# Attention and two MLP blocks on one core: bank exits on ScalarE, two-sided values and VectorE sums for batch 3, other group counts

## The chip, the cores and the metric

The kernel runs on one core of a Trainium2 chip. The metric is the device time of one execution in microseconds (us); the median of the runs counts. TensorE does the matmuls, VectorE and ScalarE the elementwise work, GpSimd a little of it, and the DMA issues stand on SyncE's queue (SP).

## What is computed

```python
scores = cap * np.tanh(scale * (q @ k.T) / cap)          # 4 batches, 12 heads, 448 tokens, 64 per head
attn = exp(scores - max(scores)); attn /= sum(attn) + 1e-9
x = attn @ v                                             # heads side by side: 448 x 768
x = x + relu(layer_norm(x) * g_ln @ w_ch1) @ w_ch2       # first MLP, 768 -> 3072 -> 768
u = x + (relu(x.T @ w_tok1) @ w_tok2).T                  # tokens mixed, 448 -> 256 -> 448
y = u + relu(u @ w_ch1) @ w_ch2                          # second MLP, 768 -> 1536 -> 768
```

All of it is float32 at the precision of a split product: an operand is written as a high part in the fp32r form and a low part, and a product is three matmuls (high x high, low x high, high x low).

## The kernel before

Activations lie transposed, with the 768 channels in six blocks of 128 partitions and the 448 tokens of a batch in the free dimension. A planner (`Program`) holds every step with the engines that may do it, an estimated cost and a key; it walks through a simulated time in which each engine takes, of the steps that are ready, the one with the lowest key, and so writes out the order of each engine's queue. The keys come from start times and paces such as `T_ATT3` and `PACE3` (head h of batch 3 has key T_ATT3 + h * PACE3); a lower key goes first, but an engine with nothing else to do takes a later one early.

Order of the work: batch 0's attention and layer norm, batch 1's attention beside one group of batch 0's first MLP alone (N0), and then MLP groups of batches 0 and 1 in pairs, into which batch 2's attention is woven. The first MLP has 6 groups of 512 hidden units, the second 3. A pair group applies the weights of one group to both batches; a lone group loads the same weights for one batch. The groups that are done alone stand beside the token mixing: while one batch is mixed, the other has work. With n lone groups for one batch, the other batch has the same n alone later. N1 is that number for the first MLP of batches 2 and 3, and N2 for the second MLP of both pairs. Batch 3's attention is woven into the token mixing and the second MLP of batches 0 and 1 and has to be done ahead of the pair groups of batches 2 and 3.

Weights come as raw 64-bit words. The first time a group is used, `piece` turns its words into floats and splits them (L272 to L280, two steps on ScalarE, four or five on VectorE), and the split weights are written back to memory; later uses load these (`split<-kept`). Three buffers hold split weights. All loads stand on SP's queue in the planner's order.

A head (`head`, L334): scores to a bank pair (L363), tanh (L366) and exp (L367) on ScalarE, the maxima over queries by a transposed reduction on VectorE (L371, L374). For batches 2 and 3 the exponentials are then split into `eh` and `el` (L389, L391 to L396), 896 columns at a time, and the values too: `vs` holds in 160 columns the high values (64), ones (32) and the low values (64). The values matmuls (L402, L404, L405) add into one bank: rows 0 to 63 are the head's output, rows 64 to 95 the sum of the exponentials, from the ones. The keys come in 3.5 blocks of 128; in the fourth the 64 keys stand twice, and `el` holds there low parts in one half and high parts in the other. L409 takes the sums out of the bank, L412 copies the output to `x`. `divide` gathers sums and maxima of six heads and scales `x`.

The MLP: L563 and L568, L569 (hidden units, split as they leave the bank), L584 and L588 (output, added to `x`). The tokens: L615 to L665. The layer norm: L460 to L508; `normalise`: L516 to L520.

Of the kernel before, what the change touches and what calls it, by code (L numbers as in the profile page):

```python
# [14 lines left out]
AF = mybir.ActivationFunctionType  # L15
# [5 lines left out]
P = 128  # L21
# [36 lines left out]


URGENT, SCORES, PREPARE, LOAD = 1000.0, 19.31, 4.58, 24.58  # L60
N0, N1, N2 = 1, 2, 2
T_LN0, T_LN1 = 7.69, -20.0
T_AHEAD, N_AHEAD, AHEAD_PACE = 14.0, 1, 5.0
T_ALONE, STRETCH0, T_PAIR, STRETCH1 = 85.0, 1.3, 165.0, 1.14
T_ATT2, PACE2, T_ATT3, PACE3 = 171.18, 25.0, 560.0, 30.0
LEAD, RAW_AHEAD, EVACUATE, TOKENS_AHEAD = 6.3, 9.57, -7.49, 17.25


# [80 lines left out]
def block_kernel(ctx: ExitStack, tc: tile.TileContext, qkv, cap, gln, w1, w2, wt1, wt2, con, out):  # L149
# [67 lines left out]

    VS = boxes("vs", 1, [4, DV + D], F32R)
    EH, EL = boxes("eh", 1, [2, S], F32R), boxes("el", 1, [2, S], F32R)
    M = boxes("m", 2, [2, 2, NJ])  # L220
    rs_t, rm_t = [place(f"rs{i}", [H, NJ]) for i in range(2)], [place(f"rm{i}", [H, NJ]) for i in range(2)]
    RS = [[Box(t[:, 6 * g:6 * g + 6]) for g in range(2)] for t in rs_t]
    RM = [[Box(t[:, 6 * g:6 * g + 6]) for g in range(2)] for t in rm_t]
# [101 lines left out]

    def attention(b, start, pace):
        x = x_t[b]
        early = b < 2
        rs, rm = rs_t[b % 2], rm_t[b % 2]
        qks, vls = ring(QK + lent_qk[b]), ring(V + lent_v[b])  # L330
        es = ring(lent if early else OWN)
        ms, scs = ring(M), ring(SC)

        def head(h):  # L334
            grp = h // 6
            pr, hh = divmod(h, 2)
            qk, v, m = next(qks), next(vls), next(ms)
            add("dma", 480, lambda: nc.sync.dma_start(out=qk.at, in_=qkv[b, h, :, :S + 4 * P]), (), [qk], early=LOAD)
            add("dma", 192, lambda: nc.sync.dma_start(out=v.at, in_=qkv[b, h, :, S + 4 * P:].rearrange("p (c d) -> p c d", c=4)), (), [v], early=LOAD)
            q, k = qk.at[:, :S], qk.at[:, S:]  # L340
            if not early:

                (ks,), (qs,), (vs,), (eh,), (el,) = KS, QS, VS, EH, EL
                add("act", 4 * P, lambda: act(ks.at, k, AF.Copy), [qk], [ks], early=PREPARE)  # L344
                add("dve+/pool+", 4 * P, lambda e: low(engine_of[e], ks.at[D:], k[D:], ks.at[D:]), [qk], [ks], early=PREPARE)
                add("act/dve*+", S, lambda e: copy(e, qs.at[:, 0], q), [qk], [qs], early=PREPARE)
                add("dve+/pool+", S, lambda e: low(engine_of[e], qs.at[:, 1], q, qs.at[:, 0]), [qk], [qs], early=PREPARE)

            E = []
            for half in range(2):  # L350
                sc, eb = next(scs), next(es)
                e, eb = eb.at, [eb]
                E.append((e, eb))

                def scores(half=half, sc=sc):
                    for i in range(2):
                        c, rows = 2 * half + i, slice(i * D, (i + 1) * D)
                        if early:

                            mm(sc.at[:, i, :S], k[rows, c * P:(c + 1) * P], q[rows], start=True, stop=True)  # L360
                        else:
                            for j in range(2):
                                mm(sc.at[:, i, :S], ks.at[:, c * P:(c + 1) * P], qs.at[:, j], start=j == 0, stop=j == 1)  # L363

                add("pe", (6 if early else 4) * S, scores, [qk] if early else [ks, qs], [sc], early=URGENT + SCORES)
                add("act", 2 * S, lambda e=e, sc=sc: act(e, sc.at[:, :, :S], AF.Tanh, scale=tsc), [sc], eb)  # L366
                add("act", 2 * S, lambda e=e: act(e, e, AF.Exp, scale=cap_t), (), eb)  # L367

            for half in range(2):
                e, eb = E[half]  # L370
                add("dve", 2 * S, lambda half=half, e=e: dve.tensor_reduce(  # L371
                    m.at[:, half].rearrange("p c j -> p (c j)"), e.rearrange("p c (j i) -> p (c j) i", i=32),
                    axis=AX.X, op=ALU.max, apply_transpose=True), eb, [m])
            add("dve", 4 * NJ, lambda: dve.tensor_reduce(  # L374
                rm[:, h], m.at.rearrange("p a c j -> p j (a c)"), axis=AX.X, op=ALU.max), [m], [RM[b % 2][grp]])
            po = next(head_banks)
            if early:
                def values():
                    for c in range(4):
                        n = P if c < 3 else D  # L380
                        mm(po.at[:DV, :S], v.at[:n, c], E[c // 2][0][:n, c % 2], start=c == 0, stop=c == 3)  # L381

                add("pe", 15 * S, values, [v, *E[0][1], *E[1][1]], [po], early=URGENT)
            else:
                add("act", 4 * D, lambda: act(vs.at[:, :, :D], v.at[:, :, :D], AF.Copy), [v], [vs])
                add("dve+", 4 * D, lambda: low(dve, vs.at[:, :, DV:], v.at[:, :, :D], vs.at[:, :, :D]), [v], [vs])
                for half in range(2):
                    e, eb = E[half]
                    add("act", 2 * S, lambda e=e: act(eh.at, e, AF.Copy), eb, [eh])  # L389
                    if half == 0:  # L390
                        add("dve+", 2 * S, lambda e=e: low(dve, el.at, e, eh.at), [eh, *eb], [el])  # L391
                    else:
                        add("dve+", S, lambda e=e: low(dve, el.at[:, 0], e[:, 0], eh.at[:, 0]), [eh, *eb], [el])

                        add("dve+", S, lambda e=e: dve.scalar_tensor_tensor(
                            el.at[:, 1], eh.at[:, 1].bitcast(F32), neg, e[:, 1], op0=ALU.mult, op1=ALU.add), [eh, *eb], [el])  # L396

                    def values(half=half):
                        for i in range(2):
                            c = 2 * half + i  # L400
                            if c < 3:
                                mm(po.at[:DV, :S], vs.at[:, c, :DV], eh.at[:, i], start=c == 0, stop=False)  # L402
                            n, part = (P, eh) if c < 3 else (D, el)
                            mm(po.at[:D, :S], vs.at[:n, c, DV:], part.at[:n, i], start=False, stop=False)  # L404
                            mm(po.at[:DV, :S], vs.at[:, c, :DV], el.at[:, i], start=False, stop=c == 3)  # L405

                    add("pe", (6 - half) * S, values, [vs, eh, el], [po], early=URGENT)

            add("dve", S, lambda: dve.tensor_reduce(  # L409
                rs[D:DV, h], po.at[D:DV, :S].rearrange("p (j i) -> p j i", i=32),  # L410
                axis=AX.X, op=ALU.max, apply_transpose=True), [po], [RS[b % 2][grp]])
            add("dve", S, lambda: dve.tensor_copy(x[hh * D:(hh + 1) * D, pr], po.at[:D, :S]), [po], [X[b][pr]])  # L412

        def divide(grp):

# [274 lines left out]
    with tc.manual_schedule():  # L690
        setup()
        prog.key = T_AHEAD
        for g in range(N_AHEAD):
            prepare(g)
        prog.key = 0.0
        attention(0, 0.0, 3.97)
        prog.key += T_LN0
        layer_norm(0)
        normalise(0)
        head_banks = side_banks = ring(BANKS[:2])  # L700
        attention(1, 60.01, 6.39)
        prog.key += T_LN1
        layer_norm(1)
        normalise(1)
        head_banks = side_banks = ring(BANKS[:1])

        main_banks = ring(BANKS[2:])
        n0, n1, n2 = N0, N1, N2
        prog.key, stretch = T_ALONE, STRETCH0
        weave(mlp(groups((0,), 0, n0)))  # L710
        main_banks = chain(BANKS[2:], ring(BANKS[1:]))
        attention(2, T_ATT2, PACE2)
        layer_norm(2)
        attention(3, T_ATT3, PACE3)
        prog.key, stretch = T_PAIR, STRETCH1
        weave(mlp(groups((0, 1), n0, NG1 - n0)))
        weave(tokens(0, HIDDEN[2]), mlp(groups((1,), 0, n0)), ahead=TOKENS_AHEAD)
        weave(tokens(1, HIDDEN[2]), mlp(groups((0,), NG1, n2)), ahead=TOKENS_AHEAD)
        weave(mlp(groups((0, 1), NG1 + n2, NG2 - n2), (0,)))
        weave(mlp(groups((1,), NG1, n2), (1,)))  # L720
        normalise(2)
        stretch = 1.0
        weave(mlp(groups((2,), 0, n1)))
        layer_norm(3)
        normalise(3)
        weave(mlp(groups((2, 3), n1, NG1 - n1)))
        weave(tokens(2, HIDDEN[2]), mlp(groups((3,), 0, n1)), ahead=TOKENS_AHEAD)
        weave(tokens(3, HIDDEN[2]), mlp(groups((2,), NG1, n2)), ahead=TOKENS_AHEAD)
        weave(mlp(groups((2, 3), NG1 + n2, NG2 - n2), (2,)))
        weave(mlp(groups((3,), NG1, n2), (3,)))  # L730
        prog.emit()
# [41 lines left out]
```

## Time and profile before

| | us |
|---|---|
| median of 3 runs | 1416.29 |
| lowest, highest | 1415.66, 1422.54 |
| the profiled execution | 1421.1 |
| its span, first to last instruction | 1419.3 |
| TensorE busy in it | 1389.8 |
| VectorE busy in it | 889.8 |
| ScalarE busy in it | 599.4 |

The rows further down come from the profiled execution, with times counted from the start of its span. A group of instructions has a line of the kernel, an engine, an operation, what it writes and reads, a count, its busy time and the mean of one in ns. The ends of matmuls are modelled and overlap; the distance from one start to the next tells what one costs.

### The profile page before, as it was taken

Reading aid. Unit: us, or ns where it says so; the run is one execution under the profiler, and the core shown is the slowest. Engines: PE = TensorE matmul, PEld = TensorE weight load, DVE = VectorE, ACT = ScalarE, POOL = GpSimd, SP = SyncE. Lnnn points to the kernel's source line nnn. Section 1 sums busy time; section 2 is a strip of 40 time slices with the busy share of each in tenths; the row PEclk is TensorE's granted clock in tenths of the full one; section 3 lists DMA queues with packets and bytes.
Section 4 is the critical chain, followed back from the end, with each engine's and each line's share of the span. In section 5 each row is a group of like instructions: output and inputs, shape, how many; then the busy total and the mean of one; then the engine's idle time right before and its main releaser. Section 6 shows DMA issues by size and latency. Waiting matters only on the chain.

```text
span 1419.3 us, 17844 instructions
## 1 busy us (share of the span) xinstructions
PE 1389.8 (98%) x6560; PEld 1179.0 (83%) x6560; DVE 889.8 (63%) x1589; ACT 599.4 (42%) x961; POOL 66.2 (5%) x51
## 2 busy tenths in 40 slices
PE   8979989999999999999999999999999999999998
PEld 3326578889898998887888889999999999999997
DVE  6999799889998998799997771221212223333221
ACT  8976567666766646776664320001010011211000
POOL 0000001110111001100000000000000000000000
PEclk9989999999999999999999999999999999999999
DMA  8784447667576756568875566523324245454366
GB/s 279 263 272 140 140 133 228 206 216 245 170 227 211 232 165 221 156 214 266 258 248 189 171 212 215 176 96 97 127 82 129 90 147 170 161 178 148 117 196 196
DMA packets 135672, 262.18 MB, mean 185 GB/s; under 512 B 10144, under 2 KB 72864, under 8 KB 135584
## 3 DMA queue, kind: packets, MB, share of 16 engines
q1 hardware_dynamic: 135008, 260.74, 56.6%
q8 instruction: 52, 0.85, 0.2%
q10 hardware_dynamic: 576, 0.29, 0.1%
q14 instruction: 36, 0.29, 0.1%
HBM read 198.86 MB, written 62.13 MB: 184 GB/s over the span
## 4 chain that ended last, share of the span: by engine, by line
PE 89%; DVE 7%; DMA 2%; ACT 1%; issue 1%; SPq 0%; ACTq 0%; DVEq 0%
PE bank L584 36%; PE bank L563 36%; PE sc L363 3%; PE bank L381 3%; PE bank L639 2%; PE bank L658 2%; PE bank L405 2%; PE bank L404 2%; PE sc L360 1%; PE bank L402 1%; DVE m L371 1%; DVE split L169 1%; DMA split<-kept 1%; DVE whole L276 1%; PE bank L615 1%
## 5 line engine op out<-in xcount | busy, mean ns | idle before, releaser
L563 PE MATMUL bank<-big,split 128*128 128x448 f32 x2592 | 551.4, 369 | 4.8 <-DVE split L169 2.6
L584 PE MATMUL bank<-h,split 128*128 128x448 f32 x2592 | 550.0, 368 | 2.1 <-DVE split L169 0.9
L563 PEld LDWEIGHTS bank<-big,split 128*128 128x128 f32 x2592 | 485.4, 188 | 54.7 <-DVE split L169 4.2
L584 PEld LDWEIGHTS bank<-h,split 128*128 128x128 f32 x2592 | 484.7, 188 | 48.3 <-issue 2.0
L568 ACT ACTIVATE h<-bank 128x448 fp32r<-128x448 f32 x144 | 78.4, 545 | 423.6 <-PE bank L563 423.2
L588 DVE TENSOR_TENSOR x<-x,bank 128x448 f32<-128x448 f32 x216 | 133.2, 618 | 187.5 <-PE bank L584 185.8
L569 DVE SCALAR_TENSOR_TENSOR h<-bank,h 128x448 fp32r<-128x448 f32 x144 | 89.3, 620 | 203.9 <-ACT h L568 203.7
L273 ACT ACTIVATE whole<-raw 128x384 f32<-128x384 f32 (+2 forms) x130 | 77.9, 601 | 56.7 <-DVE split L169 48.0
L277 DVE CUSTOM_DVE_ANT_0 whole<-raw,whole 128x768 uint16<-128x768 uint16 (+2 forms) x130 | 83.3, 641 | 0.5
L276 DVE SCALAR_TENSOR_TENSOR whole<-raw,whole 128x384 int32<-128x384 int32 (+2 forms) x130 | 81.8, 630 | 0.2
L169 DVE TENSOR_TENSOR split<-whole,split 128x384 fp32r<-128x384 f32 (+1 forms) x126 | 80.0, 636 | 2.0 <-ACT split L173 1.6
L173 ACT ACTIVATE split<-whole 128x384 fp32r<-128x384 f32 (+1 forms) x97 | 54.7, 566 | 56.0 <-PE bank L584 27.6
L274 ACT ACTIVATE raw<-raw 128x384 int32<-128x384 uint32 (+2 forms) x130 | 77.7, 598 | 0.0
L169 POOL TENSOR_TENSOR ks<-area,ks 64x512 fp32r<-64x512 f32 x24 | 36.7, 1529 | 690.2 <-ACT ks L344 670.6
L366 ACT ACTIVATE area<-sc,tsc 128x896 f32<-128x896 f32 x48 | 48.2, 1005 | 26.1 <-DVE el L169 15.5
L366 ACT ACTIVATE x<-sc,tsc 128x896 f32<-128x896 f32 x48 | 47.7, 997 | 22.6 <-DVE m L371 8.5
L371 DVE TRANSPOSE_TENSOR_REDUCE m<-x 128x28 f32<-128x896 f32 x48 | 52.3, 1098 | 7.7 <-ACT x L367 7.5
L371 DVE TRANSPOSE_TENSOR_REDUCE m<-area 128x28 f32<-128x896 f32 x48 | 52.9, 1102 | 6.1 <-ACT area L367 5.9
L275 DVE TENSOR_SCALAR whole<-whole 128x384 int32<-128x384 int32 (+2 forms) x130 | 55.2, 427 | 1.9 <-ACT whole L273 1.7
L367 ACT ACTIVATE area<-area,cap_t 128x896 f32<-128x896 f32 x48 | 49.9, 1040 | 0.7
L367 ACT ACTIVATE x<-x,cap_t 128x896 f32<-128x896 f32 x48 | 49.6, 1037 | 0.9
L389 ACT ACTIVATE eh<-area 128x896 fp32r<-128x896 f32 x48 | 45.3, 944 | 7.6 <-PE bank L404 7.3
(107 smaller groups left out, 1112.6 us busy)
## 6 DMA issues: line engine op xcount, KB each, us to landing
split<-kept SPq DMA_DIRECT2D x136, 384.0 KB, 4.1
split<-kept SPq DMA_DIRECT2D x102, 512.0 KB, 3.6
raw<-in_w SPq DMA_DIRECT2D x72, 384.0 KB, 3.5
kept<-split SPq DMA_DIRECT2D x72, 384.0 KB, 3.5
raw<-in_w SPq DMA_DIRECT2D x54, 512.0 KB, 4.4
kept<-split SPq DMA_DIRECT2D x54, 512.0 KB, 3.8
area<-in_qkv SPq DMA_DIRECT2D x38, 480.0 KB, 4.4
area<-in_qkv SPq DMA_DIRECT2D x35, 192.0 KB, 3.7
```

The lines of the kernel that those rows point to most:

```text
L169: eng.tensor_tensor(out, whole, high.bitcast(F32), op=ALU.subtract)
L273: add("act", m, lambda: act(f.bitcast(F32), hi.bitcast(F32), AF.Copy, scale=2.0 ** -112), [r], [w])
L276: add("dve+", m, lambda: dve.scalar_tensor_tensor(f, hi, -(1 << 31), f, op0=ALU.bitwise_and, op1=ALU.bitwise_or), [r], [w])
L277: add("dve+", m, lambda: dve.tensor_tensor(f, f, lo, op=ALU.add), [r], [w])
L366: add("act", 2 * S, lambda e=e, sc=sc: act(e, sc.at[:, :, :S], AF.Tanh, scale=tsc), [sc], eb)
L367: add("act", 2 * S, lambda e=e: act(e, e, AF.Exp, scale=cap_t), (), eb)
L371: add("dve", 2 * S, lambda half=half, e=e: dve.tensor_reduce(m.at[:, half].rearrange("p c j -> p (c j)"), e.rearrange("p c (j i) -> p (c j ...
L563: mm(ph.at[:, :S], w[:, wi, cc * P:(cc + 1) * P], src[cc].at[:, xi], start=(cc, n) == (0, 0), stop=(cc, n) == (NCC - 1, 2))
L568: add("act", S, lambda ht=ht, ph=ph: act(ht.at[:, 0], ph.at[:, :S], AF.Relu), [ph], [ht], early=EVACUATE)
L569: add("dve", S, lambda ht=ht, ph=ph: dve.scalar_tensor_tensor(ht.at[:, 1], ph.at[:, :S], 0.0, ht.at[:, 0].bitcast(F32), op0=ALU.max, op1=A ...
L584: mm(py.at[:, :S], w[:, wi, i * P:(i + 1) * P], h[i].at[:, hi], start=(i, n) == (0, 0), stop=(i, n) == (G - 1, 2))
L588: add("dve", S, lambda x=x, py=py: dve.tensor_tensor(x.at, x.at, py.at[:, :S], op=ALU.add), [py], [x], early=EVACUATE)
```

## The change

Four things change. For the heads of batches 0 to 2 the copy of the output out of the bank goes from VectorE to ScalarE. For batch 3 (`BESIDE`) high and low values lie side by side in 128 columns, without the ones: for even heads high in columns 0 to 63 and low in 64 to 127, for odd heads the other way round. Each matmul then gives both products at once, in the two halves of the bank: two matmuls for each full block (`eh` and `el`), one for the fourth (`el`). The low x low product, which was left out, is now part of it. The two halves are added on the way out: ScalarE copies the half of the low values to where the exponentials of the second half lay, and VectorE adds it to the other half and writes `x`. The sums of the exponentials come from two transposed sums on VectorE, one addition for the half block and a reduction over three blocks. For the group counts, N1 goes from 2 to 3, and the second MLP of batches 0 and 1 has 1 lone group for each (N20) and 2 pair groups, where it had 2 and 1. Batch 3's heads get keys from 500 on, 40 apart, for 560 and 30.

```diff
-N0, N1, N2 = 1, 2, 2
+BESIDE = (3,)
+N0, N1, N20, N2 = 1, 3, 1, 2
-T_ATT2, PACE2, T_ATT3, PACE3 = 171.18, 25.0, 560.0, 30.0
+T_ATT2, PACE2, T_ATT3, PACE3 = 171.18, 25.0, 500.0, 40.0
...
-    M = boxes("m", 2, [2, 2, NJ])
+    M, N = boxes("m", 2, [2, 2, NJ]), boxes("n", 1, [2, 2, NJ])
...
-                add("act", 4 * D, lambda: act(vs.at[:, :, :D], v.at[:, :, :D], AF.Copy), [v], [vs])
-                add("dve+", 4 * D, lambda: low(dve, vs.at[:, :, DV:], v.at[:, :, :D], vs.at[:, :, :D]), [v], [vs])
+                vh, vl = (slice(0, D), slice(DV, DV + D)) if not beside else (slice(hh * D, hh * D + D), slice(D - hh * D, P - hh * D))
+                add("act", 4 * D, lambda: act(vs.at[:, :, vh], v.at[:, :, :D], AF.Copy), [v], [vs])
+                add("dve+", 4 * D, lambda: low(dve, vs.at[:, :, vl], v.at[:, :, :D], vs.at[:, :, vh]), [v], [vs])
...
+                            if beside:
+                                for part in (eh, el) if c < 3 else (el,):
+                                    mm(po.at[:, :S], vs.at[:, c, :P], part.at[:, i], start=c == 0 and part is eh, stop=c == 3)
+                                continue
...
-                    add("pe", (6 - half) * S, values, [vs, eh, el], [po], early=URGENT)
+                    add("pe", ((4 if beside else 6) - half) * S, values, [vs, eh, el], [po], early=URGENT)
+            if beside:
+                other, n = Box(E[1][0][:, 1], E[1][1]), next(sums)
+                for half in range(2):
+                    e, eb = E[half]
+                    add("dve", 2 * S, lambda half=half, e=e: dve.tensor_reduce(
+                        n.at[:, half].rearrange("p c j -> p (c j)"), e.rearrange("p c (j i) -> p (c j) i", i=32),
+                        axis=AX.X, op=ALU.add, apply_transpose=True), eb, [n])
+
+                add("dve", 3 * NJ, lambda: dve.tensor_tensor(n.at[:D, 0, 0], n.at[:D, 0, 0], n.at[:D, 1, 1], op=ALU.add), (), [n])
+                add("dve", 3 * NJ, lambda: dve.tensor_reduce(
+                    rs[:, h], n.at.rearrange("p a c j -> p j (a c)")[:, :, :3], axis=AX.X, op=ALU.add), [n], [RS[b % 2][grp]])
+                mine, others = slice(hh * D, (hh + 1) * D), slice((1 - hh) * D, (2 - hh) * D)
+                add("act", S, lambda: act(other.at[mine], po.at[others, :S], AF.Copy), [po], [other])
+                add("dve", S, lambda: dve.tensor_tensor(x[mine, pr], po.at[mine, :S], other.at[mine], op=ALU.add), [po, other], [X[b][pr]])
+                return
...
-            add("dve", S, lambda: dve.tensor_copy(x[hh * D:(hh + 1) * D, pr], po.at[:D, :S]), [po], [X[b][pr]])
+            add("act", S, lambda: act(x[hh * D:(hh + 1) * D, pr], po.at[:D, :S], AF.Copy), [po], [X[b][pr]])
...
-        weave(tokens(1, HIDDEN[2]), mlp(groups((0,), NG1, n2)), ahead=TOKENS_AHEAD)
-        weave(mlp(groups((0, 1), NG1 + n2, NG2 - n2), (0,)))
-        weave(mlp(groups((1,), NG1, n2), (1,)))
+        weave(tokens(1, HIDDEN[2]), mlp(groups((0,), NG1, N20)), ahead=TOKENS_AHEAD)
+        weave(mlp(groups((0, 1), NG1 + N20, NG2 - N20), (0,)))
+        weave(mlp(groups((1,), NG1, N20), (1,)))
```

## Rows read from the trace of the kernel before

**Rows 1.** The page, busy time of each engine with share of span.

```profile
PE 1389.8 (98%) x6560; PEld 1179.0 (83%) x6560; DVE 889.8 (63%) x1589; ACT 599.4 (42%) x961; POOL 66.2 (5%) x51
```

**Rows 2.** Windows: stretch, length, busy us (count) by engine, granted clock, DMA share, GB/s.

```profile
7.00:92.00 85.00, 76.19 (x246) 29.70 (x242) 79.22 (x145) 74.61 (x98) 0.00 (x0) 0.99 0.85 286
92.00:170.00 78.00, 74.64 (x257) 38.35 (x257) 69.04 (x121) 50.72 (x62) 2.54 (x2) 0.92 0.51 155
205.00:575.00 370.00, 370.00 (x1807) 328.96 (x1806) 332.23 (x589) 240.83 (x394) 43.44 (x30) 1.00 0.64 208
575.00:705.00 130.00, 126.21 (x635) 111.27 (x634) 121.26 (x234) 90.31 (x160) 11.33 (x7) 1.00 0.72 232
705.00:774.00 69.00, 69.00 (x337) 61.83 (x336) 60.58 (x102) 40.11 (x65) 8.32 (x6) 1.00 0.67 220
774.00:845.00 71.00, 70.77 (x345) 61.82 (x344) 55.93 (x106) 25.27 (x40) 0.00 (x0) 1.00 0.58 185
845.00:905.00 60.00, 59.29 (x288) 53.55 (x287) 12.16 (x20) 4.37 (x8) 0.00 (x0) 1.00 0.68 221
```

**Rows 3.** The chain of waits: start, us, what; the first pair group of batches 2, 3.

```profile
905.14 29.76 PE bank L563 x144
```

**Rows 4.** Timeline of TensorE, second and first half of two heads' values: start, us, instruction.

```profile
584.64 0.36 PE L402 MATMUL bank<-eh,vs 128*96 128x448 f32 x1
...
585.34 0.41 PE L404 MATMUL bank<-el,vs 64*64 64x448 f32 x1
585.68 0.44 PE L405 MATMUL bank<-el,vs 128*96 128x448 f32 x1
585.96 1.40 PE L584 MATMUL bank<-h,split 128*128 128x448 f32 x6
...
590.50 0.36 PE L402 MATMUL bank<-eh,vs 128*96 128x448 f32 x1
...
591.70 1.18 PE L584 MATMUL bank<-h,split 128*128 128x448 f32 x5
```

**Rows 5.** Windows of L412 alone, the last step of a head, in batch 3.

```profile
540.00:605.00 65.00, 3.08 (x5) 1.00 0.58 189
605.00:770.00 165.00, 2.47 (x4) 1.00 0.72 236
770.00:810.00 40.00, 1.85 (x3) 1.00 0.52 163
```

**Rows 6.** Groups by line over the whole span: count, busy us, mean ns, idle before.

```profile
L584 PEld LDWEIGHTS bank<-h,split 128*128 128x128 f32 x2592 | 484.7, 188 | 48.3 <-issue 2.0 <-DVE split L169 1.3 <-ACT split L173 1.2
...
L371 DVE TRANSPOSE_TENSOR_REDUCE m<-area 128x28 f32<-128x896 f32 x48 | 52.9, 1102 | 6.1 <-ACT area L367 5.9
...
L409 DVE TRANSPOSE_TENSOR_REDUCE rs<-bank 32x14 f32<-32x448 f32 x48 | 31.1, 648 | 17.6 <-PE bank L405 13.1 <-PE bank L381 2.8 <-PE sc L360 0.7
L412 DVE COPY x<-bank 64x448 f32<-64x448 f32 x48 | 29.6, 617 | 0.9
...
L405 PEld LDWEIGHTS bank<-el,vs 128*96 128x96 f32 x96 | 15.4, 161 | 9.9 <-issue 5.1
...
L374 DVE TENSOR_REDUCE rm<-m 128x14 f32<-128x56 f32 x48 | 11.4, 237 | 0.1
...
L472 ACT ACTIVATE mean<-bank 128x448 f32<-128x448 f32 x4 | 2.2, 546 | 5.4 <-PE bank L471 5.4
```

**Rows 7.** Timeline of TensorE from 640 to 680: matmuls after a wait, in brackets.

```profile
646.48 3.88 PE L584 MATMUL bank<-h,split 128*128 128x448 f32 x18 [0.89 <-DVE x L588]
...
667.49 1.50 PE L658 MATMUL bank<-t,h 128*128 128x448 f32 x6 [0.97 <-DVE h L569]
...
678.67 1.28 PE L584 MATMUL bank<-h,split 128*128 128x448 f32 x5 [0.94 <-DVE split L169]
```

**Rows 8.** Who waited for whom to 125 us: us in total, times, longest.

```profile
PEld sc L360 <- ACT x L366: 17.5, 12, 4.0
```

**Rows 9.** Line 519, the normalised values' high copies, 800 to 850: first and last start.

```profile
L519 ACT ACTIVATE big<-area x8: 577/578/581, 803.4 to 843.0; 128x448 fp32r<-128x448 f32 x8
```

More of the change, by code (lines that the diff above doesn't have):

```diff
@@ L327, in attention @@
         x = x_t[b]
-        early = b < 2
+        early, beside = b < 2, b in BESIDE
         rs, rm = rs_t[b % 2], rm_t[b % 2]
@@ L331, in attention @@
         es = ring(lent if early else OWN)
-        ms, scs = ring(M), ring(SC)
+        ms, scs, sums = ring(M), ring(SC), ring(N)
         def head(h):
```

## The prediction

> **What bounds the kernel now.** I read the page's busy shares first, then the windows by stretch, then the chain of waits, then single instructions. The shares make TensorE the suspect: 98% of the span against 63% for VectorE [rows 1]. The windows say where that is true [rows 2]. From 205 to 575 us TensorE is busy without a gap. From 575 to 705 it is busy for 126.21 of 130 us while VectorE is at 93% of its time; this is the stretch of the token mixing and of the lone second-MLP groups whose weights are still being split. From 705 to 845 only 0.2 us are missing, although VectorE is still at 79 to 88%. After 845 VectorE has almost nothing to do and TensorE is full to the end. Before 92 us three engines are close together: TensorE 76, VectorE 79, ScalarE 75 of 85 us.
>
> In the quiet part 144 matmuls take 29.76 us, 206.7 ns each [rows 3]. That is the price of a matmul here, and the way to read the end: a matmul that disappears in a stretch where TensorE never waits brings the end 0.2 us nearer.
>
> **The values matmuls of batch 3.** Now a head has 6 in the first half and 5 in the second. The first six start at 590.50 and the next work starts at 591.70: 1.20 us. The second five run from 584.64 to 585.96: 1.32 us, more than 5 x 0.2, because around the one on 64 rows the starts are 0.34 us apart (585.34 to 585.68) [rows 4]. Together 2.52 us. After the change a head has 4 and 3, all on 128 rows and 128 columns: 7 x 0.2067 = 1.45 us (7 x 0.200 = 1.40 at the pitch of the first six). Saved: 1.07 us a head, 12.9 us for 12 heads. All heads lie between 540 and 810 us [rows 5], where TensorE is 97 to 100% busy, so I take it whole. Lower bound: if the 3 heads of the thinnest part save nothing, 9.6 us.
>
> The weights get wider, 128 columns for 96 and 64. A load of 128 columns takes 188 ns, one of 96 takes 161 [rows 6], and both lie inside the pitch of 200 to 207 ns, so I cost them at nothing; their cover is the matmul before them. The Trainium skill (TensorE: Matmul & The Clock Gate, section "The mechanism" of Part 3) says that a weight load overlaps running matmuls only where it goes to other rows of the array. By that rule the loads would count too: some 1.66 us before (estimate, 134 ns for 64 columns by the step from 128 to 96) and 1.32 after, so the saving would be 4.1 us larger over 12 heads. The trace does not agree: loads of 188 ns on all 128 rows fit into a pitch of 206.7.
>
> **VectorE and ScalarE.** The copy out of the bank costs VectorE 0.617 us [rows 6]; for the 36 heads of batches 0 to 2 it goes to ScalarE, where the same kind of copy from a bank costs 0.546: VectorE -22.2 us, ScalarE +19.7. For a head of batch 3 VectorE gets two transposed sums over 128x896 (taken as the maximum of the same shape, 1.10 us each), a small add (no row of that form; between 0 and the 0.237 of the small reduction, I take that as the nearest), a small reduction (0.237) and an add out of the bank in place of the copy (0.617 for 0.617), and loses the transposed reduction of the bank (0.648): 2.20 + 0.24 + 0.24 - 0.65 = +2.0 us, 24 us for 12 heads. ScalarE gets one copy, 0.55 us a head. In sum VectorE stays as it is, but 22 us leave the first 575 us and 24 us come in where batch 3 runs.
>
> **Does that hold up TensorE?** The places where it waits for VectorE now are between 640 and 680 us, 0.89, 0.97 and 0.94 us among them [rows 7]; in all 3.8 us are lost from 575 to 705. There two lone groups of the second MLP split fresh weights. The change leaves one there and makes the other a pair group, with 29.8 us more of matmuls (144 x 206.7 ns) over the same splitting. From 575 to 774 VectorE works 181.8 of 199 us, 91%. Afterwards the same content lasts about 221 us (+29.8, less 7 heads of 1.07) and asks for 181.8 + 9 x 2.0 + 6.2 (ten evacuations of 0.62) = 206 us, 93%. So it is not relieved on the whole, but its worst part is. I take back 2 us of the 3.8 (bounds: all of it, or 2 us more lost).
>
> **Batch 3's heads take longer.** The sums and the two-step exit read the exponentials again and write into their second box, so the next head's tanh, which is behind them in ScalarE's queue, waits for them. Now three heads finish in the 40 us from 770 to 810, 13.3 us each [rows 5]; two sums, two small operations and a copy make it about 16.5. Behind a waiting head load on SP's queue stand the weight loads of the lone groups. With the extra lone group of the first MLP the heads run beside lone groups for longer: those move 221 GB/s at a DMA share of 0.68 and lose 0.7 of 60 us today [rows 2]. I put 1.5 us on this (0 to 4). The matmuls are as many with 3 lone groups and 3 pairs as with 2 and 4, and the number of group loads stays at 25 (one more in the first MLP, one less in the second), so that itself costs nothing; the cover is the DMA's spare 32%, and without it each load late by a microsecond is one lost.
>
> **The start.** VectorE has the copies among its work to 92 us, 7.4 of its 79 us; ScalarE would go from 75 to 81 of 85 us. The fullest engine is then as full as before (95% for 93%), with the splitting copies free to change sides. TensorE waits here for the tanh (17.5 us of weight loads' waits in 12 pieces, the longest 4.0 [rows 8]). I take 0, between -5 and +5. Batches 1 and 2 have ScalarE at 65% and TensorE at 96 to 100% [rows 2], so nothing is gained or lost there.
>
> **Sum:** -12.9 - 2 + 1.5 + 0 = -13.4 us. The profiled execution took 1421.1 us (span 1419.3), 4.8 above the median of the runs, 1416.3. On its own time it gives 1407.7; less the same 4.8 this is 1402.9, and I say 1403.
>
> **Rivals.** *VectorE swallows it.* If VectorE is what limits 575 to 774 us as a whole, and not only the part where the waits show, the 18 us that nine heads add there are paid in full, and of 12.9 saved and a stretch with some slack little remains: about 1412. For it: 93% in the first window, 0.9 us waits released by VectorE. Against it: from 205 to 575 VectorE is at 90% and TensorE loses nothing.
>
> *ScalarE becomes the bound of the start.* 81 of 85 us, and its queue is in order, so a copy that waits for the last values matmul holds the tanh behind it. The granted clock there is 0.92 on the mean from 92 to 170 us [rows 2], that is, part of it at 1.2 instead of 2.4 GHz after TensorE had waited; 8% missing of 78 us is 12.5 us at the lower level. Three us more of waiting and as many lost to a longer slow part: +6, 1409. By the Trainium skill (same page, Part 1, "What's actually happening") the slow clock is the default and only activity lifts it; the trace agrees in so far as of the stretches read the clock is below 1 only in the two where TensorE waited most, before 170 us [rows 2].
>
> *Batch 3 comes too late* (slower). The pair groups of batches 2 and 3 need batch 3's normalised values. Now its last head leaves its bank at about 806 us and the last normalised copy ends at 843 [rows 5, 9], 62 us ahead of the pair groups at 905 [rows 3]. With the change there are four lone groups (119 us) between the last pair of batches 0 and 1 and that point; 37 us go to the division and the normalising, so 82 us hold five heads of 16.5. If seven are left over, TensorE stands 33 us: 1435. It decides from six left over on. For it: the heads' keys are 40 apart and end later than before. Against it: nine heads are out by 774 us today, when by their keys about five were due [rows 5].
>
> **Chances.** The forecast 0.68; VectorE swallows it 0.14; the start 0.12; late batch 3 0.06. The forecast's own range is 1393 to 1410 (values -9.6 to -13.3, the other terms' bounds taken together rather than all at one end); with the first two rivals 1393 to 1413. About 0.5%, 7 us, is what a measurement can tell from no change: faster 0.77 (the forecast and most of the start's case), same 0.16, slower 0.07.
>
> **What will show it.** Right, if the values line has 84 matmuls for batch 3 at 0.2 us, if 575 to 705 loses less than 3.8 us, if the quiet part from the first pair group of batches 2 and 3 to the end keeps 206.7 ns a matmul and only shifts. Wrong, if TensorE's windows between 575 and 850 show more waits for VectorE than now, if the stretch to 120 us is longer by more than 3 us, or if TensorE stands ahead of the pair groups.

## The result and the profile after

The changed kernel takes 1399.4 us in the median of 4 runs (1397.6 to 1400.8), the kernel before 1417.2 beside it (1415.7 to 1422.5): 17.8 us less, a ratio of 0.986 with the interval 0.984 to 0.989. The forecast was 1403 us, 13.4 us less. The profiled execution took 1399.1, its span is 1397.3.

The page's first part, and windows with the columns of [rows 2]:

```profile
PE 1370.9 (98%) x6512; PEld 1178.4 (84%) x6512; DVE 887.7 (64%) x1602; ACT 612.0 (44%) x995; POOL 63.2 (5%) x52
```

```profile
7.00:92.00 85.00, 79.23 (x250) 31.62 (x248) 76.02 (x138) 81.26 (x112) 0.00 (x0) 0.98 0.87 285
92.00:170.00 78.00, 74.94 (x273) 40.57 (x274) 65.23 (x117) 51.33 (x71) 2.41 (x2) 0.97 0.52 162
205.00:575.00 370.00, 370.00 (x1814) 331.78 (x1813) 333.54 (x600) 246.03 (x405) 44.65 (x32) 1.00 0.66 212
575.00:705.00 130.00, 125.55 (x633) 115.13 (x632) 121.68 (x228) 87.29 (x154) 10.13 (x8) 0.99 0.62 204
705.00:774.00 69.00, 69.00 (x339) 63.17 (x338) 61.91 (x118) 43.88 (x73) 5.36 (x4) 1.00 0.62 203
774.00:845.00 71.00, 71.00 (x352) 64.71 (x351) 59.27 (x112) 23.01 (x38) 0.00 (x0) 1.00 0.64 206
```

Against [rows 1, 2]: 48 matmuls fewer, VectorE the same in total, ScalarE 13 us more. ScalarE fills the start as forecast (81.26 of 85 us). From 575 to 705 TensorE still loses 4.4 us where it lost 3.8. So the gain is not a relieved VectorE there. (A window is a stretch of time; the change stands some microseconds further on in its work at the same time.)

The new instructions, groups by line (columns as in [rows 6]); L408 are batch 3's values matmuls, L421 the transposed sums, L425 and L426 the small steps, L429 and L430 the exit, L436 the exits of the other batches:

```profile
L421 DVE TRANSPOSE_TENSOR_REDUCE n<-area 128x28 f32<-128x896 f32 x24 | 26.3, 1097 | 0.0
L436 ACT ACTIVATE x<-bank 64x448 f32<-64x448 f32 x36 | 19.3, 535 | 23.1 <-DVE rs L433 9.2 <-PE sc L363 5.2 <-PE bank L384 5.1
L408 PE MATMUL bank<-el,vs 128*128 128x448 f32 x48 | 15.6, 366 | 0.0
L408 PE MATMUL bank<-eh,vs 128*128 128x448 f32 x36 | 13.1, 365 | 0.0
L430 DVE TENSOR_TENSOR x<-bank,area 64x448 f32<-64x448 f32 x12 | 7.3, 612 | 1.3 <-ACT area L429 1.1
L429 ACT ACTIVATE area<-bank 64x448 f32<-64x448 f32 x12 | 6.5, 540 | 17.1 <-PE bank L408 16.7 <-DVE n L421 0.2
L425 DVE TENSOR_TENSOR n<-n 64x14 f32<-64x14 f32 x12 | 2.8, 237 | 0.0
L426 DVE TENSOR_REDUCE rs<-n 128x14 f32<-128x42 f32 x12 | 2.3, 189 | 0.0
```

The 84 matmuls are there. From start to next start they take 17.1 us in sum, and the 132 of the trace before 30.4. That is the 13 us of the forecast. The other durations are within 0.05 us of those taken.

One more thing differs, and it is not the change's. In the pair groups of batches 2 and 3 the matmuls stand 202.7 ns apart until 1087 us (144 in 29.18 us), where [rows 3] has 206.7; the granted clock is 1.00 in both. From 1274 us on they are at 206.7 again, as the kernel before is from 1296. The chain of waits, start, us, what:

```profile
916.15 29.18 PE bank L587 x144
...
1273.89 29.76 PE bank L587 x144
```

Of the 22.0 us between the two spans this stretch accounts for some 4. The MLP matmul with which the pair groups begin in the kernel before comes 18.2 us earlier in the change (there, with one lone group more, a lone group begins with it, at 887 us), and the one 1008 MLP matmuls later 21.8 us earlier. The second profile of the kernel before, below, shows that this belongs to an execution, not to a kernel.

### The profile page after: what moved, and what is told of

Its sections match the earlier page's. It is cut to its first block, busy times and chain, and to the rows that moved or that the text cites. A ratio compares the mean times of both kernels' runs of the same rounds, so it can differ in the third digit from the quotient of the medians.

```text
span 1397.3 us, 17773 instructions
## 1 busy us (share of the span) xinstructions
PE 1370.9 (98%) x6512; PEld 1178.4 (84%) x6512; DVE 887.7 (64%) x1602; ACT 612.0 (44%) x995; POOL 63.2 (5%) x52
## 4 chain that ended last, share of the span: by engine, by line
PE 89%; DVE 6%; ACT 3%; DMA 1%; issue 1%; SPq 0%; ACTq 0%; DVEq 0%
PE bank L587 37%; PE bank L608 37%; PE sc L366 3%; PE bank L384 3%; PE bank L682 2%; PE bank L663 2%; PE bank L408 1%; PE sc L363 1%; DVE m L374 1%; ACT x L369 1%; PE bank L414 1%; PE bank L413 1%; PE bank L466 1%; ACT x L370 1%; PE bank L639 1%
## 5 line engine op out<-in xcount | busy, mean ns | idle before, releaser
L176 ACT ACTIVATE split<-whole 128x384 fp32r<-128x384 f32 (+1 forms) x85 | 47.9, 564 | 43.6 <-PE bank L608 19.7
L172 POOL TENSOR_TENSOR ks<-area,ks 64x512 fp32r<-64x512 f32 x23 | 31.7, 1377 | 675.5 <-ACT ks L347 675.5
```

The costliest lines, as they stand in the source:

```text
L172: eng.tensor_tensor(out, whole, high.bitcast(F32), op=ALU.subtract)
```

## The experiments

Times are medians, beside runs of the kernel before on the same chip (1416.8 for the first four, 1417.3 for the next four, 1416.0 for the last). In the rest, "lost" is the time of a window in which TensorE is not busy.

**The three parts, each alone, and the change without the values.** The exits on ScalarE for all 48 heads, batch 3's too (in the change batch 3 has the two-step exit), nothing else:

```diff
-            add("dve", S, lambda: dve.tensor_copy(x[hh * D:(hh + 1) * D, pr], po.at[:D, :S]), [po], [X[b][pr]])
+            add("act", S, lambda: act(x[hh * D:(hh + 1) * D, pr], po.at[:D, :S], AF.Copy), [po], [X[b][pr]])
```

> The kernel before with one edit: the exits of all 48 heads go to ScalarE. The prediction's theory (the start is balanced, TensorE is full afterwards): 1417, within 5 us. The rival that ScalarE becomes the bound of the start: first MLP matmul over 3 us later than 119.2 and 1423. What the trace after suggests (the first MLP matmul later, the normalisation of batch 1 earlier): 3 us gained by 231 us, 1414.

The values side by side alone: the changed kernel with these constants, and with the exits of batches 0 to 2 on VectorE as before.

```diff
-N0, N1, N20, N2 = 1, 3, 1, 2
+N0, N1, N20, N2 = 1, 2, 2, 2
...
-T_ATT2, PACE2, T_ATT3, PACE3 = 171.18, 25.0, 500.0, 40.0
+T_ATT2, PACE2, T_ATT3, PACE3 = 171.18, 25.0, 560.0, 30.0
```

> The kernel before with batch 3's values side by side and its sums on VectorE; exits of batches 0 to 2 on VectorE, group counts and keys as before. The prediction's theory (TensorE is the bound, the matmuls saved count whole): 12.9 less, 1404. The rival that VectorE swallows it (24 us more work between 540 and 810 us): 1412 to 1417, with TensorE losing over 10 us from 575 to 845.

The group counts and batch 3's keys alone (with `BESIDE = ()` and the exits on VectorE), and the changed kernel with the values alone taken back:

```diff
-BESIDE = (3,)
+BESIDE = ()
```

> The kernel before with the group counts (N1 3, N20 1) and the keys of batch 3 (500, 40) of the change, and nothing else. The prediction's theory: the same matmuls, 2 us of VectorE's waits back and 1.5 lost, 1417. The rival that the worst stretch for VectorE being thinned out is what brings the gain: 1408 or less, with nearly no waits of TensorE from 575 to 705.

> The changed kernel with the side-by-side values taken back (exits on ScalarE for all heads, group counts and keys as changed). The prediction's theory: 12.9 more than the change, 1412. If the gain comes from the exits and the groups instead: 1405 or less. If only the three parts together work, VectorE being short without the other two: also 1412, but the run with the side-by-side values alone is then at 1412 or more.

Measured: the exits alone 1410.8, ratio 0.996 (0.994 to 0.998); the values alone 1409.2, 0.995 (0.994 to 0.997); groups and keys alone 1413.0, 0.997 (0.995 to 0.999); the change without the values 1409.3, 0.995 (0.993 to 0.997). So 6.0, 7.6 and 3.8 us, 17.4 in sum, each good to some 2 or 3 us. Alone the values bring less than their 12.9, and the exits bring 6 where 0 was forecast. The window from 575 to 705 with the values alone:

```profile
575.00:705.00 130.00, 122.37 (x614) 110.81 (x613) 122.62 (x236) 90.05 (x163) 10.59 (x8) 0.99 0.71 235
```

and with groups and keys alone:

```profile
575.00:705.00 130.00, 128.81 (x648) 114.34 (x647) 118.60 (x219) 87.84 (x154) 13.66 (x10) 1.00 0.64 204
```

The values alone lose 7.6 us there for 3.8 before. The two longest waits in their timeline of TensorE are for the addition to `x`, VectorE's exit of the MLP:

```profile
642.14 7.68 PE L608 MATMUL bank<-h,split 128*128 128x448 f32 x30 [3.64 <-DVE x L612]
...
693.22 2.70 PE L608 MATMUL bank<-h,split 128*128 128x448 f32 x12 [2.17 <-DVE x L612]
```

So part of the rival "VectorE swallows it" is real: some 4 us of the 12.9 go there. At the end of the longer wait the granted clock also went to its lower level for some microseconds (mean 0.83 in this window):

```profile
640.00:650.00 10.00, 7.86 (x34) 7.20 (x35) 8.60 (x18) 3.66 (x7) 0.00 (x0) 0.83 0.79 265
```

The groups alone do the contrary: 1.2 us lost for 3.8, 2.6 back, where the forecast took 2.

**The values and the exits together, without groups and keys.** The changed kernel with the two lines of constants of before.

> The changed kernel with group counts and keys of before: side-by-side values and exits on ScalarE, without the third part. If the parts simply add up (7.1 us from the values alone, 5.8 from the exits alone): 1404. If the values give all of their 12.9 us only where VectorE is relieved, and it is the group counts that relieve it: 1404 or more, with the waits of TensorE for VectorE from 600 to 700 us still 5 us or more. If the exits relieve it: 1399.

1400.8, ratio 0.988 (0.985 to 0.990), 16.5 us less, and close to the change with all three parts. The two alone bring 13.6 in sum; the difference of 2.9 us lies inside the intervals, so that they do more together than in sum is not shown. On top of the exits the values bring 10.0 us (1410.8 to 1400.8); on top of exits and groups 9.9 (1409.3 to 1399.4). Groups and keys bring 1.4 us on top of the rest, no more than the change's own two medians differ (1399.4, and 1397.6 below). The forecast for them was half a microsecond. The waits for VectorE from 575 to 705 are not gone (125.43 of 130 us busy), but in the timeline of TensorE none is for an addition to `x` any more, where the values alone had 3.64 and 2.17 us; the longest is 0.98 us, and the granted clock stays at 1.00.

**The sums made twice.**

```diff
-                for half in range(2):
+                for half in (0, 1, 0, 1):
                     e, eb = E[half]
                     add("dve", 2 * S, lambda half=half, e=e: dve.tensor_reduce(
...
```

> The changed kernel with the transposed sums of batch 3 made twice, four in place of two for each head: 26 us more on VectorE between 540 and 800 us, nothing else. If VectorE has room there (93% by the prediction's sum): 26 us do not fit into 221 x 7% = 15 us, so some 10 us more, 1409. If VectorE is the bound of the whole stretch (the rival): 26 more, 1425. If TensorE alone is the bound: 1399.

1397.2, ratio 0.985 (0.983 to 0.987): not slower than the change. The 26 us of sums cost nothing. By the pages VectorE's total rises by 21.5 us, not 26 (909.2 for 887.7), and 8 us of batch 3's normalising move behind 850 us, where VectorE has little to do: its last high copy starts at 860.9 us for 843.7 in the change. So what the run loads onto the stretch itself is less than its expectation says. The window from 575 to 800 of the change:

```profile
575.00:800.00 225.00, 220.55 (x1097) 202.28 (x1096) 207.62 (x384) 140.87 (x240) 15.48 (x12) 0.99 0.62 202
```

and of this kernel:

```profile
575.00:800.00 225.00, 223.31 (x1116) 204.85 (x1115) 212.65 (x382) 142.17 (x239) 16.03 (x12) 1.00 0.63 207
```

VectorE is at 94.5% of the window and TensorE loses less than in the change, 1.7 us for 4.4. My own sum (26 us into 15 us of room) was wrong too: a busy share says nothing of who waits. The sums are needed only by the division behind the sixth head, and the planner lays them where VectorE has nothing more urgent. I take it that what costs TensorE is how long an MLP exit stands behind other work, which changes with the order the planner finds; the waits named in the traces fit that, but no run varies it alone. That the run is 2 us ahead of the change is not the sums' doing either: in its profile it is already some 20 matmuls ahead at 231 us (808 for 788), though the orders of the two are the same up to 503 us.

**Batch 2's values side by side as well.**

```diff
-BESIDE = (3,)
+BESIDE = (2, 3)
```

> The changed kernel with batch 2's values side by side as well: 48 matmuls fewer between 200 and 490 us, 24 us more on VectorE there, which stands at 90% of 370 us now and at 88% without batch 2's exits. If TensorE is the bound there as in batch 3's stretch: 9 to 13 us less than the change, 1388. If VectorE is full there (88% and 24 us more is 95%, with conversions that TensorE needs): 1399 or more, with waits for VectorE between 205 and 550 us where there are none now.

1398.0, ratio 0.987 (0.985 to 0.989): no faster than the change, though 48 more matmuls are gone. The window from 205 to 490 of the change:

```profile
205.00:490.00 285.00, 285.00 (x1387) 253.86 (x1386) 254.88 (x456) 191.58 (x317) 37.05 (x26) 1.00 0.68 219
```

and of this kernel:

```profile
205.00:490.00 285.00, 277.80 (x1352) 253.39 (x1351) 269.19 (x485) 190.27 (x318) 32.78 (x23) 0.99 0.66 217
```

TensorE loses 7.2 us in a stretch where it lost none. VectorE is at 94.5%, the same share as with the doubled sums, and here it does cost. TensorE's waits in this window, with who ended them (us in total, times, longest):

```profile
PE bank L608 <- DVE x L612: 3.9, 5, 1.1
PE sc L366 <- ACT area L369: 3.2, 3, 2.4
```

In batch 2's stretch the rival holds: most of what the matmuls save turns into waits for the additions to `x` and for the tanh.

**Where the exits' gain lies.** Batch 0's exits alone on ScalarE (for batch 1's the condition is `b == 1`):

```diff
+            if b == 0:
+                add("act", S, lambda: act(x[hh * D:(hh + 1) * D, pr], po.at[:D, :S], AF.Copy), [po], [X[b][pr]])
+            else:
+                add("dve", S, lambda: dve.tensor_copy(x[hh * D:(hh + 1) * D, pr], po.at[:D, :S]), [po], [X[b][pr]])
```

> The kernel before with the exits of batch 0's 12 heads alone on ScalarE. All 48 exits there gave 5.8 us, and the trace puts it ahead of 190 us, with 86 matmuls from 92 to 120 us for 68. If batch 0's exits bring it (VectorE freed where it stands at 93%): 1413, most of the gain. If ScalarE becomes the bound to 92 us (the prediction's rival): 1417 to 1420.

> The kernel before with the exits of batch 1's 12 heads alone on ScalarE, where VectorE works 69 of 78 us and ScalarE 51. If the gain is that of the maxima that come earlier beside batch 0's layer norm: 1413, with the granted clock from 92 to 120 us nearer to 1 than 0.79. If batch 0's exits bring it: 1417.

1417.7, ratio 1.000 (0.998 to 1.002), and 1422.3, ratio 1.003 (1.001 to 1.005): at the end neither brings anything, the second is slightly slower. Both of my guesses fall. But the time at the end hides the start. TensorE's matmuls by 231 us, in the kernel before, with all exits on ScalarE, in the change, with batch 0's exits there and with batch 1's:

```profile
0.00:231.00 231.00, 210.32 (x774) 118.91 (x775) 205.12 (x380) 166.00 (x229) 5.60 (x10) 0.96 0.63 206
0.00:231.00 231.00, 210.80 (x794) 121.40 (x795) 198.16 (x364) 177.19 (x257) 8.59 (x12) 0.99 0.66 210
0.00:231.00 231.00, 213.24 (x788) 121.79 (x789) 196.29 (x362) 176.09 (x254) 9.16 (x12) 0.98 0.66 209
0.00:231.00 231.00, 214.07 (x778) 122.03 (x779) 201.46 (x372) 169.47 (x240) 5.60 (x10) 0.95 0.64 207
0.00:231.00 231.00, 209.82 (x783) 119.47 (x784) 199.83 (x371) 170.24 (x240) 5.47 (x10) 0.97 0.63 207
```

The five traces of kernels whose order begins as in the kernel before have 766 to 776 matmuls there, the six whose order begins as in the change 788 to 808; the means differ by 21, some 4 us. Batch 0's exits alone lie barely above the first group, batch 1's between the two. Batch 1's then lose it again: from 575 to 705 TensorE is busy for 125.01 us, with a wait of 2.88 us at 648 us for a splitting copy. And the times of these two kernels spread over 8 us each (1411.9 to 1420.7, and 1415.7 to 1424.0); the profile of the first has the spacing of 206.7 ns in the quiet stretch, as the first profile of the kernel before, and took 1420.0 for 1421.1. A gain of a microsecond or two with batch 0's exits is not excluded. With all exits there, the rest of the 6 us lies from 575 to 705 (127.97 us busy for 126.21), where that run also has batch 3's exits on ScalarE. The window from 92 to 120, where batch 0 is normalised and batch 1's heads run, first in the kernel before:

```profile
92.00:120.00 28.00, 24.64 (x68) 10.11 (x69) 25.80 (x52) 20.01 (x26) 0.00 (x0) 0.79 0.53 165
```

with all exits on ScalarE:

```profile
92.00:120.00 28.00, 25.73 (x86) 9.97 (x86) 26.26 (x50) 23.38 (x33) 0.00 (x0) 0.98 0.64 202
```

in the change:

```profile
92.00:120.00 28.00, 26.34 (x82) 10.24 (x82) 25.18 (x48) 22.40 (x31) 0.00 (x0) 0.93 0.61 196
```

with batch 0's exits there:

```profile
92.00:120.00 28.00, 25.89 (x70) 10.59 (x68) 24.41 (x47) 18.47 (x24) 0.00 (x0) 0.80 0.56 177
```

and with batch 1's:

```profile
92.00:120.00 28.00, 25.05 (x74) 9.24 (x74) 25.64 (x48) 23.98 (x33) 0.00 (x0) 0.86 0.58 187
```

With both batches' exits on ScalarE TensorE does 82 to 86 matmuls there for 68, at a granted clock of 0.93 to 0.98 for 0.79; with one batch's 70 or 74, at 0.80 or 0.86. Who waited for whom in that window, TensorE for the tanh and the tanh for VectorE's maxima, before:

```profile
PE sc L360 <- ACT x L366: 5.7, 2, 3.6
ACT x L366 <- DVE m L371: 5.0, 4, 2.0
```

with all exits on ScalarE:

```profile
PE sc L360 <- ACT x L366: 2.3, 2, 1.4
ACT x L366 <- DVE m L371: 1.5, 1, 1.5
```

with batch 0's exits there:

```profile
PE sc L360 <- ACT x L366: 2.1, 1, 2.1
ACT x L366 <- DVE m L371: 5.7, 5, 1.8
```

and with batch 1's:

```profile
PE sc L360 <- ACT x L366: 6.0, 2, 4.7
ACT x L366 <- DVE m L371: 1.1, 3, 0.6
```

The tanh writes where VectorE's maxima still have to be read. With all exits on ScalarE it waits 1.5 us for 5.0, and TensorE waits 2.3 us for 5.7. That fits a VectorE that reaches the maxima sooner, and a TensorE that pauses less and stays longer at 2.4 GHz. One batch's exits alone shorten one of the two waits each, and the clock stays at 0.80 or 0.86. Why it takes both stays open; so does whether batch 2's exits have a part in the gain, since batch 2's alone was not tried.

**The kernel before a second time, and its output writes from another queue.**

> The kernel before, unchanged, profiled a second time. In its first profile the matmuls from 849 to 1143 us stand 206.7 ns apart, in the kernel after and in the four experiments so far 202.7 on the mean. If the distance is a state that a stretch happens to fall into, a second profile can show 202.7 there and then has a time near 1416; if it belongs to the kernel's order, it shows 206.7 again.

```diff
-                        add("dma", S // 2, lambda b=b, e=e, x=x: nc.sync.dma_start(out=out[e, :, b], in_=x.at), [x], ())
+                        add("dma", S // 2, lambda b=b, e=e, x=x: nc.scalar.dma_start(out=out[e, :, b], in_=x.at), [x], ())
```

> The kernel before with the 24 output writes issued from ScalarE's queue and not from SP's, where they wait for VectorE's last addition with weight loads behind them. TensorE's two waits for weights at 842 and 849 us (1.3 us together) should go. If it is one of these waits that leaves the matmuls behind it at 206.7 ns: 202.7 from 850 to 1143 and 6 us less, 1411. If not: 1 us less, 1416.

The second profile of the kernel before took 1415.2 us for 1421.1. Its pair groups of batches 2 and 3:

```profile
903.25 29.18 PE bank L563 x144
```

29.18 us for the 29.76 of [rows 3], in the same kernel with the same order. Its span is 1413.5, 5.8 us shorter, and all of that comes between 840 and 1143 us: 1403 matmuls in a row stand 4 ns closer, 5.6 us. Against this profile the change's span is 16.2 us shorter, not 22.0. The writes from ScalarE's queue gave 1420.3, ratio 1.002 (1.000 to 1.003). TensorE's waits for weights at 839 and 845 us are still there (0.17 and 0.58 us, for 0.23 and 0.71 in the first profile of the kernel before), so the writes alone were not their cause. The matmuls behind them stand 202.7 ns apart: such a wait alone does not set the distance to 206.7. Neither of the two expected times came.

**The change a second time**, beside the kernel with both batches side by side.

> The changed kernel unchanged, beside the run above on the same chip, and for a second profile: 1399. If the distance of the matmuls in the quiet stretches is a state that each execution falls into, it may differ from the first profile's 202.7 (850 to 1050 us) and 206.7 (1300 to 1375 us), and the share of the span at the lower clock to 120 us may differ from 6.8 us.

1397.6, ratio 0.987 (0.984 to 0.989); 202.7 ns from 885 us on as in its first profile, and two pieces at the lower clock ahead of 120 us, 3.4 and 6.8 us, where the first profile had only the one of 6.8. No kernel tried is faster than the change by more than these runs differ among themselves.

## Why the prediction held, step by step

**The values matmuls, -12.9.** The size is right (30.4 us to 17.1), "I take it whole" is not: 7.6 us come out alone and 10 beside the other parts. Alone, some 4 us are paid back from 575 to 705, mostly as waits for VectorE's additions to `x` (3.64 and 2.17 us); where the rest goes is not shown. The bound of 9.6 was nearer. By the rule of the Trainium skill weighed there (TensorE: Matmul & The Clock Gate, "The mechanism" of Part 3) the matmuls alone would have saved 17 us, an estimate; the trace has 13.3, and loads of 188 ns on all 128 rows fit into a distance of 202.7, so it does not agree. The same section of the Trainium skill also names loads into a background weight buffer as pulled ahead of running matmuls; which of the two cases a load here is, no run shows.

**VectorE and ScalarE.** +2.0 us a head on VectorE and the totals came as worked out. That its sheer amount does not hold up TensorE in batch 3's stretch is what the doubled sums say, with part of the work moved behind the stretch; that its place can, the values alone and batch 2.

**The groups.** 2 us were to come back where two lone groups split weights: alone, 2.6 of the window's 3.8; in the change itself none (4.4 lost for 3.8). The 1.5 us set aside for weight loads beside longer heads did not show; three heads still leave in the 40 us from 770 to 810.

**The start, 0.** This is the step that failed, by some 4 us: 21 matmuls more by 231 us. I compared the shares of the fullest engine (93% and 95%) and found a draw. ScalarE did become the fuller one, and the first MLP matmul came at 122.5 us for 119.2, as the rival and the sign "longer by more than 3 us" had it. But TensorE was not held up: from 7 to 120 us it had done 332 matmuls for 314. And that was not the end of the chain: the matmuls of batch 1's heads, done earlier, were missing from the next stretch, and batch 1's normalising ended earlier. Line 519, the normalised values' high copies, from 100 to 210 us, first and last start, before:

```profile
L519 ACT ACTIVATE big<-area x12: 561/574/579, 115.6 to 204.6; 128x448 fp32r<-128x448 f32 x12
```

and its counterpart after:

```profile
L543 ACT ACTIVATE big<-area x12: 572/577/579, 121.3 to 195.7; 128x448 fp32r<-128x448 f32 x12
```

Batch 0 is normalised 5.7 us later, batch 1 8.9 us earlier. The rows for it were there: the clock of 0.92 from 92 to 170 us [rows 2] and the tanh's waits [rows 8].

**The quiet part** was to keep 206.7 ns and only shift. It didn't, and for no reason in the change. This would account for the 4.8 us between the profiled execution and the median that I carried along without a cause: the first profile of the kernel before had the long distance in that stretch, and the second, without it, took 1415.2 us. The bookkeeping (-13.4 on its own time, less 4.8) was sound all the same.

**The rivals.** "VectorE swallows it": for batch 3 in part; with batch 2 as well, no time was gained. "ScalarE becomes the bound of the start": its sign came, the first MLP matmul 3.3 us later, but not its mechanism; TensorE waited less to 120 us, at a higher clock. "Batch 3 comes too late": no; its last normalised copy starts at 843.7 us, as before, and the pair groups begin at 916.

So the total is nearer than its terms, and that is partly luck: the values brought 3 to 5 us less than forecast, the exits 4 to 6 more, the groups 1 to 3 more, and these cancel in part. Of the three signs named for the forecast only the 84 matmuls at 0.2 us came; 575 to 705 lost more than 3.8 us, and the quiet part did not keep 206.7 ns. Of the three against it the one of the start came; TensorE's waits for VectorE from 575 to 850 are about as before (3.9 us for 3.7), and it does not stand ahead of the pair groups.

## What to carry to other kernels

Where an engine never waits, work taken from it comes off the end only as far as the others keep up; ask which of their steps it waits for next, not how busy they are: a VectorE busy for 94.5% of the time cost nothing in one stretch and 7 us in another. A tie of busy shares at the start is no answer; ask which wait of TensorE each engine ends there, and count the matmuls done by a time behind that stretch: a first step that comes later may mean only that other work went ahead of it. And profile the kernel before twice: a few microseconds between two executions of the same program may lie in one stretch and look like the change.

## What the runs showed of the hardware

In long rows of equal matmuls of 128x448 (128 rows, 128 columns) these stand either 206.7 ns apart, or 202.7 on the mean with most steps from 199 to 207, both at a granted clock of 1.00. A row mostly keeps the distance in which it began: 1247 matmuls at 202.7 in the change's first profile, 1403 at 206.7 in the first of the kernel before. It is no law: with both batches side by side one row goes over from 202.7 to 206.7 ns at 473 us, between equal matmuls and with no wait. The timeline of TensorE has 24 matmuls in 4.9 us from start to start, then 48 in 9.9:

```profile
467.09 5.02 PE L608 MATMUL bank<-h,split 128*128 128x448 f32 x24
471.95 10.05 PE L587 MATMUL bank<-big,split 128*128 128x448 f32 x48
481.84 0.37 PE L408 MATMUL bank<-eh,vs 128*128 128x448 f32 x1
```

The same kernel fell into either in two profiles, for 5.6 us of the 5.8 between them. Of the kernel before's 18 runs beside the first four experiments 13 lie from 1415.4 to 1417.8 and 5 from 1420.5 to 1423.8 us, which fits two distances in one stretch; that the runs without a profile differ for this reason was not shown, nor what decides which distance a stretch gets.

The start of one and the same order of work also differs from execution to execution: six traces with the same order up to 231 us have 788 to 808 matmuls done by then, at a granted clock of 0.97 to 0.99.
